# Unit 4's queries moved into unused columns of the MLP's hidden tile, and the hand-kept order of the first attention re-sorted

## The chip, the cores and the metric

The kernel runs on 1 core of one Trainium2 chip. The time is the device time of one execution in microseconds (us); a comparison takes the median of several runs. The engines are TensorE (PE; its weight loads, PEld, are listed apart), VectorE (DVE), ScalarE (ACT), GpSimd (POOL) and SyncE (SP), which here only issues DMA transfers. Each engine takes its instructions strictly in program order, and waits for other engines by semaphores.

## What is computed

Attention with normalized queries and keys for 8 batches of 12 heads (448 tokens, head size 64), then a layer norm and an MLP (multi-layer perceptron) with a residual, on 768 columns:

```python
def rmsnorm(x, g):
    return x / np.sqrt(np.mean(x * x, axis=-1, keepdims=True) + 1e-06) * g
q_n, k_n = rmsnorm(q, g_q), rmsnorm(k, g_k)
scores = q_n @ k_n.transpose(0, 1, 3, 2) / np.sqrt(64)
attn = softmax(scores)
x = (attn @ v)            # heads side by side: (8, 448, 768)
xn = (x - mean(x)) / np.sqrt(var(x) + 1e-06) * g_ln
out = x + np.maximum(xn @ w_ch1, 0.0) @ w_ch2     # 768 -> 3072 -> 768
```

## The kernel before

**Units, pairs, pieces.** Two heads make a pair, 48 pairs in all. Loads and preparation go by units of one or two pairs (`UNITS`): units 0 to 3 are batch 0 (pairs 0; 1; 2, 3; 4, 5), units 4, 5 and 6 are batch 1 (pairs 6, 7; 8, 9; 10, 11), unit 7 begins batch 2. The preparation of a unit is cut into pieces (`pieces`, from line 235), each one or a few instructions; their letters are

- `b`: takes the loaded tiles; `a`, `c`: squares of k and of q on ACT (L254); `d`, `e`: their sums by head on DVE (L257); `g`: the roots on ACT (L260, L261; `gq`, `gk` for unit 0)
- `i`: k times the gains (L271), on DVE for units 0 and 1 and on POOL after that; `j`: the high half of k in float16 (L277 on POOL for units 1 to 5, else L279 on ACT); `k`: the low half (L282, DVE)
- `l`: the scaled q (L79, DVE); `m`: its second copy (L318, POOL for units 1, 2 and 4, else DVE); `z`: the values in float16 (L324 and L330, POOL).

For a pair p, `Kp` and `Qp` transpose its keys and queries on PE into PSUM and copy them out (L360, L363, copy L365; L374, L377, copy L380 on ACT or L382 on DVE). From pair 6 on both use the one PSUM tile `tr`. `Sp.i` is one of seven score tiles (L397; L407 and L408 for the rest rows) with its exp on ACT (L413); the scores have two PSUM banks in turn. `Vp.i` multiplies such a tile with the values (L450, L452); `Vp.6` ends the pair, and DVE writes the pair's results (L465, L466, L467, L472). Pairs 1, 3 and 5 keep their sums in two of the three banks that the transposes of q, the first MLP products and psH use, too.

**The hand-kept list.** The first attention, batch 0 with the preparation of batch 1's first units and pair 6's scores, is written out by hand in `ORDER`, which `first_attention` goes through item by item. Since every engine runs in program order, this list is each engine's order. Besides the pieces it holds `Ln` (the loads of unit n, all on SP, keys first; `L8k` only the keys of unit 8), `Wn` (a third of the first weight matrix, w1, a DMA on POOL, L595), `G` and `G2` (the norm's gains), `Tp` (statistics, DVE, L625), `A`, `Nt`, `R` (aggregate, norm and root of the layer norm, L640 and L646), `Xt` (transposes of token tile t on PE, L682, copied by ACT, or by DVE for t = 2, L690), `Ut` (the first MLP products of token tile t, psU, L926; `U2` with the relu on ACT, L930) and `M` (seven small reductions on DVE).

**After the list** come the MLP of batch 0 (`first_mlp`: psH at L702, relu at L705, psC at L712) and, between its matmuls, the next batches' attention in steps that `attention` plans: the pieces of units 5 to 9 at the places in `EARLY`, less those that the list has already (`done`). `run_rest` spreads the steps evenly over the matmuls' cost. The step with unit 6's `b` also issues half of the second weight matrix.

**Buffers of the loads.** `load_unit` puts a unit's q, k and v either at a fixed place (`home`) or into one of three buffers of the pool `p_in` in turn. Fixed places lie in `hS`, the tile of the MLP's hidden layer, which nothing else uses before the MLP (4608 columns of float32; relu f writes columns 192 f to 192 f + 191), and in `free`, which is the tile `w2s` where the first batch's q and k were loaded. Before the change k4 and q4 take the first two buffers, k6 the third, and q6 the first one again, once `k4` has read it; `L8k` takes q4's. `RING` lists the tiles that go through the pool; the step that runs a unit's `k` or `l` loads the one three places on.

Of the kernel before, what the change touches and what calls it, by code (L numbers as in the profile page):

```python
# [22 lines left out]
UNITS = [(0, 0, 1), (0, 2, 1), (0, 4, 2), (0, 8, 2)]  # L23
# [10 lines left out]


ORDER = """
b0 a0 c0 L4 i0 j0 e0 k0 gq0 l0 b1 m0 a1 c1 K0 Q0 d0 G gk0 S0.0 S0.1 d1 e1 L5 i1 g1 j1 l1 k1 m1
z0 b2 a2 S0.2 d2 c2 S0.3 S0.4 K1 V0.0 e2 i2 S0.5 Q1 g2 l2 S0.6 S1.0 j2 V0.1 S1.1 S1.2 m2 b3
V0.2 a3 V0.3 k2 c3 S1.3 K2 V0.4 S1.4 z2 V0.5 Q2 S1.5 V0.6 V1.0 i3 W0 d3 e3 S1.6 V1.1 V1.2 S2.0
j3 T0 V1.3 S2.1 S2.2 Q3 V1.4 S2.3 K3 S2.4 V1.5 V1.6 S2.5 g3 z3 S2.6 V2.0 S3.0 S3.1 V2.1 k3  # L40
S3.2 b4 S3.3 V2.2 l3 a4 V2.3 m3 S3.4 V2.4 K4 S3.5 Q4 V2.5 V2.6 S3.6 Q5 S4.0 V3.0 S4.1 V3.1 i4
V3.2 d4 T1 K5 V3.3 W1 c4 V3.4 V3.5 S4.2 S4.3 V3.6 S4.4 S4.5 W2 e4 V4.0 V4.1 j4 S4.6 S5.0 k4
S5.1 g4 V4.2 l4 S5.2 V4.3 V4.4 V4.5 S5.3 K6 V4.6 z4 V5.0 S5.4 m4 b5 V5.1 G2 S5.5 L6 V5.2 S5.6
V5.3 V5.4 V5.5 Q6 a5 i5 V5.6 T3 T4 S6.0 S6.1 S6.2 S6.3 T5 S6.4 A V6.0 V6.1 N0 V6.2 N1 V6.3
S6.5 S6.6 d5 V6.4 X0 X1 U0 N2 R Q7 X2 c5 e5 j5 g5 k5 l5 z5 U1 U2 V6.5 M m5 V6.6 L7 L8k K7
""".split()
DMA_UNIT = 8
PE_SET = (DMA_UNIT + 1) % 2
# [15 lines left out]
TAIL = (11, 13, 17, 13, 17, 13, 19, 0)  # L64
FLAG_AT = (6, 30)
E_RING = 9
RING = [(u, n) for u in (4, 6, *range(DMA_UNIT, len(UNITS))) for n in "kq"]


def _rsqrt(nc, out, a, t, eps, mul=1.0):  # L70
# [17 lines left out]
class _Fast:  # L88
# [95 lines left out]
    def load_unit(self, u, which=(1, 0, 2)):  # L184
        nc = self.nc
        b, hs, m = UNITS[u]
        eng = nc.sync
        hS = self.hS.rearrange("p f n -> p (f n)").bitcast(FP32)
        home = {(4, 2): (hS, 0), (5, 0): (hS, 1920), (5, 1): (hS, 2816), (5, 2): (hS, 3712),
                (6, 2): (self.free, 3840), (7, 0): (self.free, 0), (7, 1): (self.free, 896),  # L190
                (7, 2): (self.free, 1792)}
        t = self.loads.setdefault(u, [None] * 3)
        for n in which:
            if (u, n) in home:
                x, c = home[u, n]
                t[n] = x[:, c:c + 896].rearrange("p (g d) -> p g d", d=D)
            else:
                t[n] = self.p_in.tile([128, 14, D], FP32, tag="kq", name="qk"[n])
            self.load_main(eng, n, t[n][:, 0:6 * m], b, hs, 2 * m)
            self.load_left(eng, n, t[n][:, 6 * m:7 * m], b, hs, 2 * m,  # L200
                           nc.gpsimd if (u, n) == (DMA_UNIT + 1, 1) else None)
# [327 lines left out]
    def attention(self):  # L529

        n, nu, nb0, done = B * NPAIR, len(UNITS), NPAIR, set(ORDER)
        todo = {}
        for u in range(4, nu):
            p, m = UNIT_PAIR[u], UNITS[u][2]
            if u == 4:
                continue
            plan = [(7 * (p - 4) + x, y) for x, y in PLAN]
            if u in EARLY:
                st, e = EARLY[u]
                names = ["bai", "d", "c", "e", "j", "gz", "k", "l", "m"]  # L540
                if u > DMA_UNIT:
                    names = ["bai", "d", "c", "j", "k", "e", "gz", "l", "m"]
                plan = [(st + (e - st) * x // 9, y) for x, y in enumerate(names)]
                if u >= DMA_UNIT:
                    plan += zip(TRANS_AT[u], "xyY")
            for at, names in plan:
                if self.late_v(u):
                    names = names.replace("z", "")
                todo.setdefault(at, []).extend(
                    self.prep_ops(u)[y] for y in names if y + str(u) not in done)  # L550
                for y in set(names) & set("kl"):
                    i = RING.index((u, "qk"[y == "k"])) + 3 if u != 5 and u != 7 else nu * 2
                    if i < len(RING):
                        todo.setdefault(at + (LOAD_AT[y == "l"] if u not in EARLY else 1), []).append(
                            lambda x=RING[i]: self.load_unit(x[0], ("qk".index(x[1]),)))
                if u in (6, 7) and "b" in names:
                    todo[at].append(lambda u=u: self.load_w2(u - 6))
        steps, mark = [], [0]

        for p in range(nb0, n + 1):  # L560
            for i in range(7):
                c = []
                if i == 0 and p < n and p % NPAIR == 0 and p > nb0:
                    c.append(lambda b=p // NPAIR: self.batch(b))
                c += todo.pop(7 * p + i, [])
                if p < n and f"S{p}.{i}" not in done and i < 6:
                    c.append(lambda p=p, i=i: self.scores(p, i))
                if p > nb0:
                    for x in {0: (), 1: (0, 1)}.get(i, (i,)):
                        if f"V{p - 1}.{x}" not in done:  # L570
                            c.append(lambda p=p, x=x: self.values(p - 1, x))
                if p < n and i == 6 and f"S{p}.6" not in done:
                    c.append(lambda p=p: self.scores(p, 6))
                if p > nb0 + 1 and i == 1 and (p - 1) % NPAIR:
                    c.append(lambda p=p: self.stats(p - 2))
                if p + 1 < UNIT_PAIR[DMA_UNIT]:
                    if i == 2 and f"K{p + 1}" not in done:
                        c.append(lambda p=p: self.trans_k(p + 1))
                    if i == 4 and f"Q{p + 1}" not in done:
                        c.append(lambda p=p: self.trans_q(p + 1))  # L580
                if p > nb0 and p % NPAIR == 0 and i == 6:
                    c.append(lambda p=p: self.stats(p - 1))
                if c:
                    steps.append(c)
            if p > nb0 and p % NPAIR == 0:
                mark.append(len(steps))
        return steps, mark
# [641 lines left out]
```

## Time and profile before

| | us |
|---|---|
| median of 3 runs (lowest, highest) | 590.16 (588.65, 591.14) |
| the profiled execution | 588.15 |
| its span from first to last instruction | 586.6 |
| PE busy in the span | 557.1 (95%) |
| DVE busy | 381.9 (65%) |
| ACT busy | 378.7 (65%) |
| POOL busy | 174.9 (30%) |

The profile is of one execution. Its own time is 1.55 us longer than the span, and 2.01 us shorter than the median of the runs. Busy time counts compute instructions only; the idle time before an instruction is shown in brackets with the engine that ended it. Rows in order of time give start, length, engine, line, operation and tiles; neighbouring instructions of a pipelined engine overlap by about 0.1 us in such rows. Lines are those of the kernel before; behind line 552 the changed kernel has one line more.

### The profile page before, as it was taken

How to read it: one execution, taken by the hardware profiler on the slowest of the kernel's cores; microseconds unless marked ns; L12 is line 12 of the kernel's file. 1: busy time of each engine (PE TensorE's matmuls, PEld its weight loads, DVE VectorE, ACT ScalarE, POOL GpSimd, SP SyncE). 2: the span in 40 equal slices, each digit the busy share in tenths (PEclk: the TensorE clock that was granted, in tenths of full speed). 3: DMA queues.
4: the chain of work that ended last, by engine and by line, in shares of the span. 5: the costliest groups of instructions: out<-in, count | busy, mean ns of one | idle time of the engine just before them, and what ended most of it. 6: DMA issues, size and time to landing. Idle time of an engine off the chain costs nothing.

```text
span 586.6 us, 13477 instructions
## 1 busy us (share of the span) xinstructions
PE 557.1 (95%) x5366; PEld 407.3 (69%) x5366; DVE 381.9 (65%) x832; ACT 378.7 (65%) x693; POOL 174.9 (30%) x196
## 2 busy tenths in 40 slices
PE   3777999999999999999999999999999999999995
PEld 1555566677677768777687768777787777777773
DVE  5898666699667586855757576854757744663434
ACT  5996887438786588647787489737787477323130
POOL 2854333303241520653141421643141400020000
PEclk9999999999999999999999999999999999999999
DMA  7999998948672796967753697958843480030201
GB/s 209 285 221 236 197 197 115 145 124 124 138 100 58 181 128 131 138 158 116 130 92 57 181 134 132 131 149 124 137 60 64 126 104 1 3 107 2 82 0 58
DMA packets 172664, 71.43 MB, mean 122 GB/s; under 512 B 132548, under 2 KB 167556, under 8 KB 172596
## 3 DMA queue, kind: packets, MB, share of 16 engines
q1 hardware_dynamic: 130100, 51.60, 41.8%
q0 software_dynamic: 41552, 18.29, 24.1%
q8 instruction: 43, 0.70, 0.5%
q10 hardware_dynamic: 944, 0.62, 0.4%
q14 instruction: 25, 0.20, 0.1%
HBM read 52.30 MB, written 11.01 MB: 108 GB/s over the span
## 4 chain that ended last, share of the span: by engine, by line
PE 78%; DVE 8%; ACT 3%; DMA 2%; issue 1%; SPq 0%; DVEq 0%; ACTq 0%
PE psH L779 30%; PE psP L802 28%; PE psS L397 7%; PE oA L450 4%; PE psH L702 3%; PE psC L712 2%; PE oB L452 2%; PE psS L403 1%; DVE w2s L745 1%; DMA q<-in_q_dram 1%; ACT E L413 1%; DVE stat L625 1%; DVE khl L282 1%; DVE ssq L257 1%; DVE x L467 1%
## 5 line engine op out<-in xcount | busy, mean ns | idle before, releaser
L413 ACT ACTIVATE E<-psS,rr_all 128x448 f16<-128x448 f32 x336 | 202.9, 634 | 41.3 <-PE psS L397 36.2
L779 PE MATMUL psH<-xnT,w 128*128 128x256 f16 (+1 forms) x2016 | 225.8, 261 | 0.0
L779 PEld LDWEIGHTS <-w 128*128 128x128 f16 x2016 | 172.7, 98 | 24.0 <-issue 4.8
L782 ACT ACTIVATE hS<-psH 128x512 f16<-128x512 f32 x150 | 90.0, 600 | 96.5 <-PE psH L779 92.1
L802 PEld LDWEIGHTS <-hS 128*128 128x128 f16 x1080 | 100.0, 98 | 57.5 <-issue 1.1
L802 PE MATMUL psP<-w,hS 128*128 128x384 f16 x672 | 126.8, 326 | 0.0
L397 PE MATMUL psS<-qU,kU 128*128 128x448 f16 x288 | 102.0, 356 | 9.4 <-ACT E L413 6.0
L450 PEld LDWEIGHTS <-E 128*128 128x128 f16 x1008 | 70.6, 98 | 37.2 <-issue 4.8
L271 POOL TENSOR_TENSOR k<-k,gprod 128x896 f32<-128x896 f32 x19 | 40.4, 2128 | 166.6 <-ACT khl L254 139.0
L785 DVE TENSOR_TENSOR hS<-hS 128x512 f16<-128x512 f16 (+1 forms) x119 | 56.8, 484 | 22.3 <-ACT hS L782 20.8
L802 PE MATMUL psP<-w2s,hS 128*128 128x384 f16 (+1 forms) x408 | 69.9, 321 | 0.0
L450 PE MATMUL oA<-v,E 128*128 128x65 f16 x864 | 66.7, 193 | 0.4 <-DVE x L467 0.4
L739 DVE SCALAR_TENSOR_TENSOR x<-psP,rs_all,x 128x384 f32<-128x384 f32 x60 | 36.4, 617 | 41.9 <-PE psP L802 41.2
L452 PE MATMUL oB<-v,E 128*128 128x65 f16 x288 | 51.8, 193 | 0.3
L813 POOL TENSOR_TENSOR x<-x,hS 128x384 f32<-128x384 f32 x21 | 23.4, 1127 | 84.4 <-ACT hS L881 83.8
L212 POOL DMA_DIRECT2D v<-in_v_dram x51 | 39.1, 781 | 8.9 <-PE oB L452 8.0
L397 PEld LDWEIGHTS <-kU 128*128 128x128 f16 x288 | 28.1, 98 | 16.8 <-issue 6.0
L465 DVE RECIPROCAL rec_all<-oA 128x6 f32<-128x6 f32 x48 | 9.2, 191 | 46.8 <-PE oA L450 46.7
L282 DVE TENSOR_TENSOR khl<-k,khl 128x896 f16<-128x896 f32 x19 | 20.7, 1091 | 25.9 <-ACT khl L279 25.9
L881 ACT ACTIVATE hS<-hS,rs_all 128x384 f32<-128x384 f32 x27 | 14.6, 604 | 33.1 <-DVE hS L785 33.1
L452 PEld LDWEIGHTS <-E 128*128 128x128 f16 x336 | 32.5, 97 | 0.4 <-DVE xl L472 0.4
L257 DVE TENSOR_REDUCE ssq<-khl 128x14 f32<-128x896 f32 (+1 forms) x24 | 25.5, 1062 | 6.0 <-ACT khl L254 5.0
(136 smaller groups left out, 601.0 us busy)
## 6 DMA issues: line engine op xcount, KB each, us to landing
k<-in_k_dram SPq DMA_DIRECT2D x19, 384.0 KB, 3.9
q<-in_q_dram SPq DMA_DIRECT2D x19, 384.0 KB, 4.2
out_dram<-x SPq DMA_DIRECT2D x14, 384.0 KB, 3.0
w<-in_moe_w_ch_dram POOLq DMA_DIRECT2D x3, 1536.0 KB, 15.0
w<-in_moe_w_ch_dram POOLq DMA_DIRECT2D x2, 2304.0 KB, 19.5
out_dram<-x POOLq DMA_DIRECT2D x9, 384.0 KB, 3.0
v<-in_v_dram POOLq DMA_DIRECT2D x51, 64.0 KB, 4.2
qU<-qn SPq DMA_TRANSPOSE x85, 2.5
```

What stands on the lines that cost most here:

```text
L212: nc.gpsimd.dma_start(out[:, :, j, 0:D], main[:, :, j])
L257: nc.vector.tensor_reduce(out=c["ssq"][:, n], in_=c["sq", n], axis=AX.X, op=ALU.add)
L271: (nc.vector if u in DVE_KG else nc.gpsimd).tensor_tensor(out=c["t"][1], in0=c["t"][1], in1=sh.gprod.unsqueeze(1).broadcast_to([128, g, D] ...
L397: nc.tensor.matmul(ps[0][:, 0:S], c["main"][:, ts(i, 128)], c["q"][:, ts(h, S)], start=True, stop=True)
L413: nc.scalar.activation(out=o, in_=x[:, 0:S], func=AFT.Exp, scale=self.units[u][3][:, g:g + 1], bias=EXP_BIAS)
L450: nc.tensor.matmul(oA[:, t, cs], E[:, ts(t, 128)], rhs, start=(i == 0 and t == 0), stop=(i == 6 and t == 2))
L452: nc.tensor.matmul(oB[:, cs], E[:, 320:448], rhs, start=(i == 0), stop=(i == 6))
L739: self.nc.vector.scalar_tensor_tensor(out=x, in0=ps, scalar=self.rs[:, b, t:t + 1], in1=x, op0=ALU.mult, op1=ALU.add)
L779: nc.tensor.matmul(ps[:, i], sh.w1[:, dc, ts(f + i, 128)], self.xnT[:, dc, 256 - N:256], start=(i == 0 and dc == 0), stop=(i == k - 1 and ...
L782: nc.scalar.activation(out=hT[:, f:f + k], in_=ps, func=AFT.Relu)
L785: nc.vector.tensor_tensor(out=out, in0=a, in1=c, op=op)
L802: nc.tensor.matmul(bank[x][:, c], a[:, f], w[:, f, c], start=(start and f == 0), stop=(stop and f == HALF - 1))
```

## The change

- The queries of unit 4 get a fixed place in `hS`, columns 896 to 1791, between v4 and q5. So only k4 of unit 4 goes through the pool, and k6 and q6 take the second and third buffer without a wait; `L8k` follows k4 in the first.
- `RING` loses its entry for q4, and the lookup in `attention` asks whether a tile is in `RING`.
- `ORDER` gets six more items, `b6 a6 c6 d6 e6 i6` near its end, and is re-sorted as a whole. Up to the first transposes little moves. Among other moves, `i1` stands ahead of `d0`; `a4` and `c4` come later; on POOL `z3` and `W0` come ahead of `i3`, and `z4` and `W2` ahead of `j4`; on DVE pair 3's results come after `k4`, `T3` and `T4` before pair 5's results, `e5` before `X2`; on PE `V5.0` comes right after `V3.6`, `U0` after `S6.6`, and `K7` right after `U2`.

The instructions are the same in number and kind; the steps after the list lack unit 6's six pieces, and one of them, left empty, is dropped.

```diff
 ORDER = """
-b0 a0 c0 L4 i0 j0 e0 k0 gq0 l0 b1 m0 a1 c1 K0 Q0 d0 G gk0 S0.0 S0.1 d1 e1 L5 i1 g1 j1 l1 k1 m1
-z0 b2 a2 S0.2 d2 c2 S0.3 S0.4 K1 V0.0 e2 i2 S0.5 Q1 g2 l2 S0.6 S1.0 j2 V0.1 S1.1 S1.2 m2 b3
-V0.2 a3 V0.3 k2 c3 S1.3 K2 V0.4 S1.4 z2 V0.5 Q2 S1.5 V0.6 V1.0 i3 W0 d3 e3 S1.6 V1.1 V1.2 S2.0
-j3 T0 V1.3 S2.1 S2.2 Q3 V1.4 S2.3 K3 S2.4 V1.5 V1.6 S2.5 g3 z3 S2.6 V2.0 S3.0 S3.1 V2.1 k3
-S3.2 b4 S3.3 V2.2 l3 a4 V2.3 m3 S3.4 V2.4 K4 S3.5 Q4 V2.5 V2.6 S3.6 Q5 S4.0 V3.0 S4.1 V3.1 i4
-V3.2 d4 T1 K5 V3.3 W1 c4 V3.4 V3.5 S4.2 S4.3 V3.6 S4.4 S4.5 W2 e4 V4.0 V4.1 j4 S4.6 S5.0 k4
-S5.1 g4 V4.2 l4 S5.2 V4.3 V4.4 V4.5 S5.3 K6 V4.6 z4 V5.0 S5.4 m4 b5 V5.1 G2 S5.5 L6 V5.2 S5.6
-V5.3 V5.4 V5.5 Q6 a5 i5 V5.6 T3 T4 S6.0 S6.1 S6.2 S6.3 T5 S6.4 A V6.0 V6.1 N0 V6.2 N1 V6.3
-S6.5 S6.6 d5 V6.4 X0 X1 U0 N2 R Q7 X2 c5 e5 j5 g5 k5 l5 z5 U1 U2 V6.5 M m5 V6.6 L7 L8k K7
+b0 a0 L4 i0 c0 j0 e0 gq0 b1 k0 l0 m0 a1 c1 K0 i1 G d0 Q0 gk0 S0.0 L5 d1 j1 z0 b2 S0.1 e1 S0.2 g1
+k1 a2 l1 d2 K1 S0.3 c2 e2 S0.4 S0.5 m1 i2 j2 Q1 V0.0 g2 S1.0 l2 m2 z2 S1.1 S0.6 b3 S1.2 V0.1 k2
+S1.3 V0.2 z3 V0.3 V0.4 K2 c3 V0.5 V1.0 S1.4 Q2 a3 S1.5 e3 V1.1 d3 V1.2 S1.6 V0.6 S2.0 W0 V1.3 i3
+S2.1 g3 V1.4 S2.2 Q3 K3 T0 S2.3 V2.0 j3 S2.4 V1.5 V1.6 V2.1 S2.5 V2.2 S2.6 b4 S3.0 l3 V2.3 S3.1
+k3 S3.2 m3 V2.4 S3.3 V3.0 c4 S3.4 V3.1 a4 i4 Q4 K4 V2.5 V2.6 S3.5 S3.6 Q5 S4.0 d4 K5 V3.2 S4.1
+S4.2 T1 W1 V3.3 S4.3 V4.0 V4.1 V4.2 S4.4 V3.4 V3.5 S4.5 z4 W2 S5.0 j4 e4 S4.6 S5.1 k4 g4 V3.6
+V4.3 V4.4 V5.0 S5.2 b5 S5.3 l4 V5.1 m4 V4.5 K6 G2 S5.4 V5.2 L6 a5 V5.3 V5.4 T3 S5.5 V4.6 V5.5
+S5.6 T4 Q6 V5.6 S6.0 S6.1 T5 A N0 N1 S6.2 V6.0 S6.3 i5 c5 V6.1 d5 S6.4 V6.2 X0 N2 V6.3 V6.4 X1
+Q7 S6.5 S6.6 U0 e5 X2 g5 M R j5 U1 V6.5 k5 U2 K7 l5 L7 L8k b6 m5 z5 a6 c6 d6 e6 V6.6 i6
 """.split()
-RING = [(u, n) for u in (4, 6, *range(DMA_UNIT, len(UNITS))) for n in "kq"]
+RING = [(4, "k")] + [(u, n) for u in (6, *range(DMA_UNIT, len(UNITS))) for n in "kq"]
...
-        home = {(4, 2): (hS, 0), (5, 0): (hS, 1920), (5, 1): (hS, 2816), (5, 2): (hS, 3712),
+        home = {(4, 0): (hS, 896), (4, 2): (hS, 0), (5, 0): (hS, 1920), (5, 1): (hS, 2816), (5, 2): (hS, 3712),
...
-                    i = RING.index((u, "qk"[y == "k"])) + 3 if u != 5 and u != 7 else nu * 2
+                    x = u, "qk"[y == "k"]
+                    i = RING.index(x) + 3 if x in RING else nu * 2
```

## The prediction

> **What bounds the kernel now.** I read the busy shares by stage first, then the chain of work that ended last, then TensorE's waits, and then, for the first 62 us, each engine's instructions in order of time. Columns by stage: length, then busy time of PE, PEld, DVE, ACT and POOL, the clock, the DMA share, GB/s; the third line is of PE alone.
>
> ```profile
> 23.00:55.34 32.34, 24.76 (x324) 16.81 (x322) 29.89 (x66) 27.56 (x52) 19.94 (x23) 1.00 1.11 231
> 12.00:32.40 20.40, 15.13 (x155) 9.21 (x154) 17.36 (x28) 19.87 (x38) 13.86 (x17) 1.00 1.09 273
> 57.30:580.00 522.70, 519.27 (x4926) 1.00 0.63 109
> ```
>
> From 57.3 to 580 us PE is busy 519.27 of 522.70: there the time is PE's work, which the change leaves alone, and at most 3.4 us of waits. Before that, in the first attention, PE is busy 24.76 of 32.34 and waits for others: ACT until about 32 us (19.87 of 20.40), DVE from 23 us on (29.89 of 32.34). The change re-sorts just this stage, so it can gain or lose only here and at the seam to the MLP (multi-layer perceptron). The chain shows the seam (start, length, engine, tile, line):
>
> ```profile
> 46.53 2.24 DVE stat L625 x9
> ...
> 49.17 1.96 DVE xn L646 x3
> ...
> 54.74 2.01 PE psU L926 x36
> ...
> 57.49 1.96 PE psH L702 x12
> ...
> 60.56 0.67 DVE kU L365
> ```
>
> After V5's results DVE does nine statistics, the norms, and the copies; PE does U1 and U2 (psU), and at 57.49 the MLP proper (psH) starts. Then it stops once more:
>
> ```profile
> 61.27 0.36 PE L397 MATMUL psS<-qU,kU 128*128 128x448 f16 x1 [1.35 <-DVE kU L365]
> ```
>
> S7.0 waited 1.35 us for the copy that belongs to K7, which came last in DVE's queue, behind M and V6's results.
>
> **The change part by part.**
>
> *The loads.* SyncE (SP) issues in order; q6 shared a buffer with k4:
>
> ```profile
> 29.28 1.75 SPq L150 DMA_DIRECT2D k<-in_k_dram  x2
> 41.48 0.37 SPq L142 DMA_DIRECT2D q<-in_q_dram  x1
> ```
>
> ```profile
> 58.89 0.94 ACT L254 ACTIVATE khl<-k 128x896 f32<-128x896 f32 x1
> ```
>
> From 31.03 (29.28 + 1.75) to 41.48 SP issued nothing. With unit 4's queries in hS, q6 goes out at about 31, v6 after k3 has read its place, and k7, q7, v7 behind them; k8 waits for k4's buffer in place of q4's. The number of DMAs is the same. Nothing on the path gains by it: unit 6's first square, at 58.89, stands directly behind the MLP's first relu and shows no wait for data. I cost the loads at 0: issued near 31 and used near 59, they have over 20 us in hand. What they could delay is a rival below.
>
> *Unit 6's first pieces in the list.* a6 and c6 move ahead of the MLP's first relu (two squares of 0.94), d6 and e6 ahead of V6's results (two reductions), i6 to the end of the list. ACT was not holding PE there, so the squares cost 0. The reductions delay V6's results and behind them K8's copy; Q8 needs K8's copy out of the same PSUM bank. Behind K7's copy stand l5, m5, d6, e6, V6's results and K8's copy: 1.1 + 0.4 + 2.0 + 1.33 + 0.57 = 5.4 us (prices below), while PE has 6 us of MLP and scores. The margin is about 0.4 us, so I take 0 and keep +0.5 as the upper end. One step without work falls out of the MLP's pacing, so S7.0 comes after 12 psH matmuls in place of 15.
>
> *K7 early.* K7 now follows U2, and its copy follows M and k5 on DVE. It is done about 2.3 us after X2's copy, S7.0 comes about 3.7 us after it. The wait goes: **-1.35**. S7.0's exps next wait for nothing but ACT, which is free.
>
> *The re-sorted list.* The prices, DVE first (start to next start is what one costs; the rows overlap a little):
>
> ```profile
> 32.33 0.66 DVE L365 COPY kU<-tr 128x960 f16<-128x960 f16 x1
> ...
> 36.49 1.07 DVE L625 BATCH_NORM_STATS2 stat<-x 128x6 f32<-128x256 f32 x3
> 37.48 0.64 DVE L365 COPY kU<-tr 128x960 f16<-128x960 f16 x1
> 38.04 0.18 DVE L465 RECIPROCAL rec_all<-oA 128x6 f32<-128x6 f32 x1
> ...
> 39.37 1.09 DVE L257 TENSOR_REDUCE ssq<-qn 128x14 f32<-128x896 f32 x1
> 40.37 1.08 DVE L282 TENSOR_TENSOR khl<-k,khl 128x896 f16<-128x896 f32 x1
> 41.37 1.09 DVE L79 SCALAR_TENSOR_TENSOR qn<-q,rr_all 128x896 f16<-128x896 f32 x1
> ...
> 53.57 0.62 DVE L382 COPY qU<-tr 128x896 f16<-128x896 f16 x1 [0.52 <-PE tr L377]
> 54.78 0.56 DVE L690 COPY w2s<-tr 128x768 f16<-128x768 f16 x1 [0.58 <-PE tr L682]
> ```
>
> A statistic like T1 costs 0.99 (36.49 to 37.48), a copy of K or Q 0.57, one pair's results 1.33 (38.04 to 39.37), e4 or k4 1.00. Now ACT and GpSimd (POOL):
>
> ```profile
> 28.76 2.76 ACT L413 ACTIVATE E<-psS,rr_all 128x448 f16<-128x448 f32 x5
> 31.42 0.94 ACT L254 ACTIVATE khl<-k 128x896 f32<-128x896 f32 x1
> ```
>
> ```profile
> 26.02 0.89 POOL L595 DMA_DIRECT2D w<-in_moe_w_ch_dram  x1
> ...
> 32.50 2.09 POOL L271 TENSOR_TENSOR k<-k,gprod 128x896 f32<-128x896 f32 x1 [3.30 <-issue]
> 34.53 1.72 POOL L595 DMA_DIRECT2D w<-in_moe_w_ch_dram  x2
> 36.73 0.93 POOL L277 CAST khl<-k 128x896 f16<-128x896 f32 x1 [0.48 <-DVE ssq L257]
> 37.60 0.83 POOL L324 CAST v<-hS 128x768 f16<-128x768 f32 x1
> 38.38 0.64 POOL L330 CAST vl<-hS 64x128 f16<-64x128 f32 x2
> ...
> 61.98 1.51 POOL L600 DMA_DIRECT2D w<-in_moe_w_ch_dram  x1
> ```
>
> Up to m3 both lists give DVE the same work, so it stands there at 32.3 (before, K4's copy starts at 32.33). In the new list Q4, K4, V2's results, Q5, d4, K5, T1, e4 follow: four copies, 1.33, 0.99 and two reductions, 6.6 us, and some 0.3 for Q4's transposes: 39.2. Next is k4, which needs j4 from GpSimd, and here the new list puts a **new wait**. The old queue on GpSimd is i4, W1, W2, j4, z4, the new one i4, W1, z4, W2, j4. i4 waits for a4 on ACT. a4 ended at 32.36 (31.42 + 0.94); the new list has one more exp (2.76 / 5 = 0.55) and c4 (0.84 to 0.94) ahead of it on a saturated ACT, and i1, now ahead of d0 on DVE at the very start, adds 0.1 to 0.6: about 34.0. Then 2.03 + 0.86 + 1.42 + 0.86 + 0.93: j4 ends at about 40.1, k4 starts at 40.3 in place of 39.2. Behind k4 on DVE stand V3's results, l4, K6's copy; PE's V5.0 waits for the PSUM bank of V3's results, and S5.2 behind it on PE, so ACT idles too, about 2 us, which it can afford.
>
> From k4's start to the end of X2's copy DVE took 14.97 us before (40.37 to 54.78 + 0.56). In the new list the same work stands there, plus V3's results (+1.33) and e5 (+1.00), while e5 and N2 fill the two idle gaps before Q7's and X2's copies (-0.52 - 0.58): 16.2. T3 and T4 move ahead of V5's results, but DVE has no hole to put them in, so this only exchanges places. X2's copy ends at 40.3 + 16.2 = 56.5, against 55.34. U1 covers the copy as before; U2 (half of 2.01), K7 and V6.6 (0.6) follow, and U0, now behind S6.6, adds up to 0.4: the MLP starts at about 58.5 in place of 57.49, **+1.0**. Bounds of this term: 0 if k4 isn't held (39.2), -1.3 if DVE's remaining idle time goes too (29.89 of 32.34 busy, less the 1.10 already taken), +2.9 if both weight issues on GpSimd take 1.51 as the one at 61.98 does (+1.3) and a4 is 0.6 later still.
>
> **Sum**: +1.0 - 1.35 + 0 = -0.35, with ends at -2.65 and +2.05. The profiled execution took 588.15 (span 586.6 and 1.55 around it), so 587.8; it ran 2.0 under the median of the runs, 590.16, so for the median **589.8**.
>
> **A rule against the change.** Weights and loads share the DMA engines:
>
> ```profile
> DMA to landing us min/median/max: 14.6/14.6/14.6
> ```
>
> This is W0, issued at 26.0 while SP's queue was idle from 31 to 41: it lands at 40.6. In the new list it is issued near 25.4, and U0, which needs it, runs some 2 us ahead of the end of X2's copy (X2's transposes and U0's own matmuls lie between), at about 54.5. The rule stands in the Trainium skill, DMA: Bandwidth & Descriptors, section Queues, rings and completion order: each engine takes turns between the queues that have work, a packet at a time. By that rule q6 to v7, now issued from 31 on, take up to half of every engine from W0. The trace agrees that the two queues ran side by side, but has no case of five loads against W0.
>
> **The rivals.**
>
> *A: k4 isn't held, and the list closes DVE's gaps.* For it: 2.45 us of DVE idle in the first row, and T4 before V5's results. Against it: z4 and W2 do stand ahead of j4. The MLP starts between -1.3 and 0, and the wait of 1.35 goes: -1.35 to -2.65, the median 587.5 to 588.8. Behind the seam PE's other waits (522.70 - 519.27 - 1.35 = 2.08) may shrink too, which would lead down to 586. Chance 0.24, of which 0.16 is faster by over 0.5%.
>
> *B (slower): GpSimd's queue holds k4 much longer.* Place: j4 behind z4 and both issues. From 40.3 on, each us that j4 is late is a us of the whole, since DVE, and by V5.0's bank PE and ACT, stand behind k4. For it: ACT is saturated ahead of a4, an issue has taken 1.51, and DVE's in-order queue has a new neighbour at every place. Against it: all other prices would have to hold too. At k4 = 42.2 the sum is +1.55, with K8's copy +2.05; from 43.1 on it is over +2.95 (593.1). Price +2 to +5, time 592 to 595. Chance 0.20, of which 0.17 is slower by over 0.5%.
>
> *C: the first weight piece lands late.* Place: U0 and, through it, X2 and the MLP's start. Doubling 14.6 gives 25.4 + 29.2 = 54.6, just when U0 wants it, and that is the point from which it costs anything; W1 and W2 follow in the same queue but are needed only five and thirteen chunks into the MLP. Price 0 to +4, time 590 to 594. Chance 0.06, of which 0.05 is slower by over 0.5%.
>
> *D: the move does nothing.* The buffer alone is without effect on the time (costed at 0), and if K7's wait is merely replaced by Q8 waiting for K8's copy (+0.5) and the DVE sum is as above, the result is 590.3. It is part of the forecast.
>
> **How the numbers follow.** Forecast, with D, 0.50, all of it within 0.5% (2.95 us, about what a measurement of this kernel can tell from no change); A 0.24; B 0.20; C 0.06. Faster by over 0.5%: 0.16, from A. Slower: 0.17 from B and 0.05 from C, 0.22. Within: 0.50 + 0.08 + 0.03 + 0.01 = 0.62. The range reaches from A's lower half, 587.0, to B's upper half, 594.5; about 0.1 lies below and 0.08 above. Between the ends of the forecast's own sum (-2.65 and +2.05) I take -0.35, since the wait at K7 and the order on GpSimd can be read off and the rest can't.
>
> **What would show it.** Right: S7.0 without the 1.35 wait; POOL's j4 (khl) ending near 40 and DVE idle about 1 us before k4; X2's copy ending near 56.5 and psH starting near 58.5; SP issuing q6 at about 31; PE from there on as before. Wrong: DVE never idle at k4 (A); psH after 60 (B); a PE wait on a DMA at U0 (C); a wait of Q8's transposes for DVE near 64.5. What would overturn the forecast is an engine that I held to be covered, above all ACT between S5.1 and X0.

## The result, and the profile after

| | median, us (lowest, highest) | runs |
|---|---|---|
| before | 589.32 (588.61, 591.37) | 22 |
| after | 590.70 (589.89, 591.93) | 22 |

The ratio after to before is 1.0021, 95% interval 1.0013 to 1.0030: a loss of 0.8 to 1.8 us, where a gain of 0.35 was forecast. The profiled execution of the changed kernel took 590.16 us, its span 588.6; that of before took 588.15 and 586.6.

The changed kernel's VectorE at the place of the new wait (start, length, engine, line, operation, tiles, and in brackets the idle time before and who ended it), then GpSimd's j4:

```profile
38.51 1.07 DVE L257 TENSOR_REDUCE ssq<-qn 128x14 f32<-128x896 f32 x1
40.54 1.09 DVE L282 TENSOR_TENSOR khl<-k,khl 128x896 f16<-128x896 f32 x1 [0.96 <-POOL khl L277]
...
44.75 0.66 DVE L365 COPY kU<-tr 128x960 f16<-128x960 f16 x1 [0.77 <-PE tr L363]
...
46.61 0.20 DVE L465 RECIPROCAL rec_all<-oA 128x6 f32<-128x6 f32 x1 [0.22 <-PE oA L450]
```

```profile
39.57 0.93 POOL L277 CAST khl<-k 128x896 f16<-128x896 f32 x1
```

j4 ends at 40.50 and k4 starts at 40.54 after 0.96 us of waiting, as forecast (40.1, 40.3, about 1). But two more idle times follow on VectorE, 0.77 and 0.22, and both wait for TensorE. TensorE's rows of the same stretch and of the seam:

```profile
42.59 0.20 PE L452 MATMUL oB<-v,E 128*128 128x65 f16 x1 [2.17 <-DVE x L467]
...
43.86 0.85 PE L363 MATMUL tr<-id,khl 128*128 128x128 f16 x6
...
59.27 2.11 PE L703 MATMUL psH<-w2s,w 128*128 128x384 f16 x12
...
65.76 0.35 PE L397 MATMUL psS<-qU,kU 128*128 128x448 f16 x1 [0.30 <-ACT E L413]
...
67.09 0.22 PE L374 MATMUL tr<-id,qn 128*128 128x128 f16 x1 [0.98 <-DVE kU L365]
```

V5.0 waited 2.17 us for the bank of V3's results. After that wait K6's six transposes took 0.85 us; in the profile of before they take 0.50:

```profile
41.58 0.50 PE L363 MATMUL tr<-id,khl 128*128 128x128 f16 x6
```

The clock tells why (the changed kernel's length, PE busy, clock, DMA share, GB/s):

```profile
39.20:42.60 3.40, 1.22 (x19) 1.00 1.14 239
42.60:46.00 3.40, 3.11 (x31) 0.51 1.13 215
```

After 3.40 us in which PE was busy 1.22, the granted clock was half for the next 3.40. The MLP starts at 59.27; the row of the same form stands at 57.33 in the profile of before (below). S7.0's wait of 1.35 us is gone, but Q8's first transpose now waits 0.98. The chain shows what stands before it (start, length, engine, tile, line), and GpSimd's row stands beside:

```profile
60.98 2.16 DVE qn L318
63.15 1.99 DVE ssq L257 x2
...
66.06 0.29 DVE xl L472
...
66.38 0.67 DVE kU L365
67.05 0.04 issue
67.09 0.22 PE tr L374
```

```profile
60.47 2.43 POOL L271 TENSOR_TENSOR k<-k,gprod 128x896 f32<-128x896 f32 x1 [2.84 <-issue]
```

m5 (L318) is a float16 copy that took 0.38 before; here it took 2.16. It lies beside i6 on GpSimd, which ends at 62.90; m5 ends 0.24 later. The two rows of before:

```profile
58.92 0.38 DVE L318 COPY qn<-qn 128x896 f16<-128x896 f16 x1
```

```profile
59.96 2.08 POOL L271 TENSOR_TENSOR k<-k,gprod 128x896 f32<-128x896 f32 x1 [4.77 <-issue]
```

Single profiles differ at their start. TensorE runs at half speed there, which the rows show (six transposes take 0.84 us) though the windows give a clock of 1.00, and this ends between 17 and 25 us, at another time in each execution. Here are before and then run e4 (below), whose lists agree up to this point:

```profile
22.71 0.50 PE L377 MATMUL psQ<-id,qn 128*128 128x128 f16 x6
```

```profile
23.75 0.83 PE L377 MATMUL psQ<-id,qn 128*128 128x128 f16 x6
```

So the clock time at which the MLP starts is no measure of a list. The expectations below count it from the first exp. ScalarE's and TensorE's rows of before, then ScalarE's of after:

```profile
12.05 1.16 ACT L413 ACTIVATE E<-psS,rr_all 128x448 f16<-128x448 f32 x2 [0.33 <-PE psS L397]
```

```profile
57.33 2.60 PE L702 MATMUL psH<-w2s,w 128*128 128x384 f16 x15
```

```profile
11.77 1.89 ACT L413 ACTIVATE E<-psS,rr_all 128x448 f16<-128x448 f32 x3 [0.24 <-PE psS L397]
```

That is 45.28 before and 47.50 after. But the slow stretch reaches past the first exp: the same count gives 46.26 for e4. A later mark is steadier: the sum of unit 4's q squares (piece e4), which is the last instruction of VectorE ahead of k4 (L257, `ssq<-qn`; 38.51 above, 39.37 before). From its start to the MLP's, before takes 17.96 us, e4 17.95, and the changed kernel 20.76. The two orders hold different work there (pair 3's results, 1.33, stand ahead of the mark before and behind it after), so this count compares only lists of the same order.

In these two profiles the MLP starts 1.94 us later (57.33 to 59.27), and from there to the end both take 529.3 us: the 1.35 gained at S7.0, and 0.64 at two later waits for exps, are used up by Q8 (0.98, and 0.30 for an exp ahead of it) and by waits further on, which differ between executions (TensorE's idle time from 50 us behind the MLP's start on is 1.2 us before, 1.6 here and 2.4 in e5, which has the list of before). The medians say 0.8 to 1.8, so these two single profiles overstate the difference.

### The profile page after: what moved, and what is told of

It reads as the page before. It is cut to its first block, busy times and chain, and to the rows that moved or that the text cites. A ratio compares the mean times of both kernels' runs of the same rounds, so it can differ in the third digit from the quotient of the medians.

```text
span 588.6 us, 13476 instructions
## 1 busy us (share of the span) xinstructions
PE 560.7 (95%) x5366; PEld 409.4 (70%) x5366; DVE 383.2 (65%) x832; ACT 378.5 (64%) x693; POOL 175.3 (30%) x196
## 4 chain that ended last, share of the span: by engine, by line
PE 76%; DMA 10%; DVE 7%; ACT 3%; SPq 2%; issue 1%; ACTq 0%; DVEq 0%
PE psH L780 30%; PE psP L803 27%; PE psS L397 6%; DMA w2s<-in_k_dram 4%; PE oA L450 4%; DMA k<-in_k_dram 4%; PE psH L703 2%; PE psC L713 2%; PE oB L452 1%; PE psS L403 1%; DVE w2s L746 1%; DMA q<-in_q_dram 1%; ACT E L413 1%; DMA hS<-in_k_dram 1%; SPq L150 1%
## 5 line engine op out<-in xcount | busy, mean ns | idle before, releaser
L397 PE MATMUL psS<-qU,kU 128*128 128x448 f16 x288 | 103.2, 362 | 7.4 <-ACT E L413 3.9
L450 PEld LDWEIGHTS <-E 128*128 128x128 f16 x1008 | 71.8, 99 | 40.0 <-issue 6.5
L450 PE MATMUL oA<-v,E 128*128 128x65 f16 x864 | 68.3, 196 | 1.5 <-ACT E L413 1.1
L882 ACT ACTIVATE hS<-hS,rs_all 128x384 f32<-128x384 f32 x27 | 14.6, 604 | 33.1 <-DVE hS L786 33.1
L452 PEld LDWEIGHTS <-E 128*128 128x128 f16 x336 | 32.8, 98 | 2.7 <-DVE x L467 2.3
L257 DVE TENSOR_REDUCE ssq<-khl 128x14 f32<-128x896 f32 (+1 forms) x24 | 25.5, 1062 | 5.0 <-ACT khl L254 4.5
## 6 DMA issues: line engine op xcount, KB each, us to landing
w<-in_moe_w_ch_dram POOLq DMA_DIRECT2D x3, 1536.0 KB, 14.9
```

What stands on the lines that cost most here:

```text
L257: nc.vector.tensor_reduce(out=c["ssq"][:, n], in_=c["sq", n], axis=AX.X, op=ALU.add)
L397: nc.tensor.matmul(ps[0][:, 0:S], c["main"][:, ts(i, 128)], c["q"][:, ts(h, S)], start=True, stop=True)
L450: nc.tensor.matmul(oA[:, t, cs], E[:, ts(t, 128)], rhs, start=(i == 0 and t == 0), stop=(i == 6 and t == 2))
L452: nc.tensor.matmul(oB[:, cs], E[:, 320:448], rhs, start=(i == 0), stop=(i == 6))
```

## The experiments

Runs are named e0 to e12. Pieces of the list have such names too; where one is meant, the text says piece. The diffs show only the part of a line that an edit touches; e5 has the change's edits to `RING` and the lookup too.

**Theory.** The loss has two places. First, k4 waits for j4; V3's results behind it hold TensorE for 2.2 us, the clock then falls to half, and VectorE waits for the slow transposes. Second, i6, which starts as soon as a6 is done, shuts m5 out, and K8's copy comes late for Q8. Against these stands the gain at K7. **Rivals:** the loads, issued 6 us earlier, compete for the DMA engines; or the re-sorted list costs by itself, wherever these two waits are.

Each ratio is to the kernel before, with its 95% interval. "First exp to MLP" and "mark to MLP" are the two counts above in that run's profile, "Q8" is the wait of Q8's first transpose there; where S7.0 still waits, the row says so.

| run | ratio | first exp to MLP, us | mark to MLP, us | Q8, us |
|---|---|---|---|---|
| before | 1 | 45.28 | 17.96 | none; S7.0 1.35 |
| after, and e0, the same again | 1.0021 [1.0013, 1.0030], 1.0021 [1.0010, 1.0033] | 47.50, 47.83 | 20.76, 20.70 | 0.98, 0.99 |
| e1, j4 first | 0.9982 [0.9971, 0.9993] | 45.56 | 18.65 | 0.99 |
| e2, c6 first | 0.9985 [0.9975, 0.9995] | 47.79 | 20.73 | none |
| e3, both | 0.9967 [0.9954, 0.9980] | 46.27 | 18.65 | none |
| e4, before with K7 early | 0.9970 [0.9959, 0.9982] | 46.26 | 17.95 | none |
| e5, before with the buffer | 1.0004 [0.9996, 1.0013] | 45.47 | 17.96 | none; S7.0 1.35 |
| e6, unit 6 not in the list | 1.0018 [1.0007, 1.0029] | 46.63 | 19.41 | none |
| e8, V3.6 ahead of k4 | 1.0009 [0.9998, 1.0019] | 46.25 | 19.44 | 0.98 |
| e9, e1 with V6's results beside i6 | 0.9972 [0.9957, 0.9987] | 46.48 | 18.65 | none |
| e10, S5.2 ahead of V5.0 | 1.0015 [1.0002, 1.0028] | 48.22 | 20.70 | 0.99 |
| e11, e3 with S5.2 ahead of V5.0 | 0.9956 [0.9939, 0.9974] | 45.54 | 18.66 | none |
| e12, e4 with unit 6's pieces | 0.9970 [0.9953, 0.9988] | 45.27 | 17.95 | none |

Profiles of one order spread by up to 1 us in the first count (45.27 to 46.26, 45.56 to 46.48) and by under 0.1 in the second.

**e1: j4 ahead of z4 and W2** in the changed kernel.

```diff
-S4.5 z4 W2 S5.0 j4 e4 S4.6
+S4.5 j4 z4 W2 S5.0 e4 S4.6
```

> The changed kernel with j4 ahead of z4 and W2 in the list, nothing else. Theory (the neighbours in the queues): the changed kernel's DVE stood idle 0.96 us for j4, PE 2.17 us for the bank of V3's results, and K6's transposes then ran at about half speed (0.85 in place of 0.50 us), which cost DVE another 0.77. With j4 early, k4 starts at about 39.5 in place of 40.54, PE's wait is about 1.1 us, and psH starts 1.0 to 1.9 us sooner than 59.27. Q8's wait of 0.98 us stays. Ratio to the kernel before 0.999 to 1.0005, from 1.0021. Rival (DVE is full anyway; the new order, with V3's results behind k4 and e5 ahead of X2, is what costs): the gap turns up again elsewhere, psH starts within 0.3 us of 59.27, ratio 1.0015 to 1.0025.

VectorE, then TensorE, of this run:

```profile
39.03 1.07 DVE L257 TENSOR_REDUCE ssq<-qn 128x14 f32<-128x896 f32 x1
40.01 1.08 DVE L282 TENSOR_TENSOR khl<-k,khl 128x896 f16<-128x896 f32 x1
```

```profile
42.05 0.20 PE L452 MATMUL oB<-v,E 128*128 128x65 f16 x1 [1.13 <-DVE x L467]
42.77 0.50 PE L363 MATMUL tr<-id,khl 128*128 128x128 f16 x6
```

k4 follows piece e4 without a bracket, TensorE's wait is half as long, the transposes take 0.50, and VectorE has no bracket from 38 to 56 us. From the mark to the MLP it is 2.1 us less, and the ratio falls by 0.0039, 2.3 us, more than expected. m5 still takes 2.16 and Q8 still waits. The first place is shown.

**e2: c6 ahead of a6**, so that i6 starts later. **e3: e1 and e2 together.**

```diff
-b6 m5 z5 a6 c6 d6 e6 V6.6 i6
+b6 m5 z5 c6 a6 e6 d6 V6.6 i6
```

> The changed kernel with c6 ahead of a6 and e6 ahead of d6, so that GpSimd's i6, which needs a6, starts about 0.85 us later, behind the start of m5 on DVE. Theory (m5 and i6 get in each other's way): in the changed kernel m5 took 2.16 us beside i6, before it took 0.38 with GpSimd idle; here m5 is back at 0.4 us or at most 0.9, K8's copy comes about 1.5 us sooner, and Q8's wait of 0.98 us goes. psH still starts at about 59.3. Ratio 1.0000 to 1.0010, from 1.0021. Rival (what delays K8's copy is d6 and e6 ahead of it, 2.0 us, whatever m5 takes): Q8's wait stays at 0.5 us or more, ratio 1.0015 to 1.0025.

> Both edits: j4 ahead of z4 and W2, and c6, e6 ahead of a6, d6. Theory: the two gains add, psH at 57.4 to 58.3, no wait of Q8, no wait of S7.0: ratio 0.9970 to 0.9990. Rival (the two waits share one slack, or the order itself costs): ratio 0.9995 to 1.0015.

VectorE, then GpSimd, of e2:

```profile
62.19 0.39 DVE L318 COPY qn<-qn 128x896 f16<-128x896 f16 x1
62.49 1.08 DVE L257 TENSOR_REDUCE ssq<-qn 128x14 f32<-128x896 f32 x1
```

```profile
62.51 2.08 POOL L271 TENSOR_TENSOR k<-k,gprod 128x896 f32<-128x896 f32 x1 [3.68 <-issue]
```

i6 lies beside a float32 sum now; both keep their normal length, m5 has its 0.39 again, and Q8's wait is gone. The second place is shown. The ratio falls by 0.0036, 2.1 us, more than expected and more than the 1.28 us of waits that went (0.98 and 0.30); with about 0.001 on either side of each ratio the rest can hardly be told from nothing. In e2 K6's transposes still took 0.85 us. Both repairs together gain 0.0054, less than the sum of the two points, 0.0075, but by the traces just what they should: 2.1 + 1.28 = 3.4 us, where 0.0054 is 3.2.

**e4: the kernel before with K7 ahead of V6.5**, nothing else.

```diff
-U1 U2 V6.5 M m5 V6.6 L7 L8k K7
+U1 U2 K7 V6.5 M m5 V6.6 L7 L8k
```

> The kernel before with K7 moved from the end of the list to right behind U2, nothing else. Theory (the wait at K7 is a term of its own): S7.0's wait of 1.35 us goes and psH starts as before, at about 57.4: 1.2 to 1.4 us faster, ratio 0.9976 to 0.9980. Rival (the wait moves on, to Q8's transposes or to an exp, as it did in the changed kernel): 0.4 us or less, ratio 0.9993 to 1.0000.

S7.0's wait goes, a wait of 0.26 for an exp appears at 65.55, and 0.0030 is 1.8 us, a little more than the 1.35; the interval holds both. One item moved gives as much as the whole change with both repairs (e3). So the rest of the re-sorting earns nothing that these runs can tell, and, since e3 is no slower than e4, it costs nothing that they can tell either once the two places are mended. That takes out the second rival.

**e0: the changed kernel again. e5: the buffer alone**, with the list of before.

```diff
-home = {(4, 2): (hS, 0),
+home = {(4, 0): (hS, 896), (4, 2): (hS, 0),
```

> The changed kernel once more, beside the next ones. Both theories: ratio 1.0005 to 1.0035 to the kernel before; TensorE's wait of about 2.2 us for V3's results and K6's transposes of 0.85 us again, if the cause lies in the order and not in one execution. If the 0.85 was an accident of the one profile, the transposes take 0.50 here and the MLP starts about 1 us earlier after the first exp (46.5 instead of 47.5 us).

> The list of before, with unit 4's queries in hS and the loads that follow from it. Theory (the loads are hidden by some 20 us of slack and take nothing from the weights' pieces): ratio 0.999 to 1.001, the wait of 1.35 us before S7.0 still there, W0 landing in about 15 us. Rival (five loads issued from 31 to 35 us on share the DMA engines with the weight pieces or with the loads just needed, and this is part of the loss of the change): ratio 1.001 to 1.003 and a wait of TensorE or VectorE for a DMA. Other side (the loads were late before): under 0.999.

e0 repeats the ratio, the 2.17 us and the 0.85 us. e5 is 1.0004, and its interval holds 1 and reaches 1.0013, 0.8 us; the time from the mark to the MLP is that of before. That takes out the first rival, the loads, as far as this interval goes.

**e6: unit 6's pieces out of the list.**

```diff
-L7 L8k b6 m5 z5 a6 c6 d6 e6 V6.6 i6
+L7 L8k m5 z5 V6.6
```

> The changed kernel without unit 6's pieces in the list (b6, a6, c6, d6, e6, i6 go back to the pacing of the MLP). Theory (the loss at Q8 comes from m5 sharing its time with i6, which starts as soon as a6 has ended): m5 0.39 us, no wait of Q8's first transpose for VectorE, while the wait for V3's results and the late MLP stay: ratio 0.9980 to 0.9995 to the kernel before, like the run with c6 first. Rival (d6 and e6 ahead of V6's results make the wait, whatever m5 takes): the wait goes here too, but then m5 needs not be short. Other rival (unit 6's pieces in the list were worth something later in the MLP): ratio 1.001 or more.

The mechanism came as expected (m5 0.39, no wait of Q8), the time did not: 1.0018. TensorE's rows of this run from 60 to 110 us that show a wait:

```profile
65.73 0.35 PE L397 MATMUL psS<-qU,kU 128*128 128x448 f16 x1 [0.25 <-ACT E L413]
77.66 0.38 PE L403 MATMUL psS<-qU,kU 128*64 128x448 f16 x2 [0.61 <-ACT E L413]
96.08 0.35 PE L397 MATMUL psS<-qU,kU 128*128 128x448 f16 x1 [0.31 <-ACT E L413]
```

The two later waits are those of the kernel before; the changed list had put one of 0.28 in their place. In sum 1.17 here stand against 0.98 + 0.30 + 0.28 = 1.56, so this edit is worth only 0.4 us (0.0007), which these intervals can't tell from nothing. The theory had left out what comes back; the other rival of the expectation had named it.

The same profile shows what the half clock costs. The wait at V5.0 was again 2.17, but here the clock stayed at 1.00 and VectorE waited only for j4. This run's windows, then its only bracket on VectorE from 38 to 56 us:

```profile
39.80:43.20 3.40, 1.22 (x19) 1.00 1.14 230
43.20:46.60 3.40, 2.56 (x36) 1.00 1.12 219
```

```profile
41.11 1.09 DVE L282 TENSOR_TENSOR khl<-k,khl 128x896 f16<-128x896 f32 x1 [0.66 <-POOL khl L277]
```

In the executions with half clock, VectorE's two later waits are 0.77 + 0.22 (after), 0.35 + 0.55 (e0) and 0.41 + 0.56 (e2), 0.9 to 1.0 us each time; in e6 none. From the mark to the MLP e6 takes 19.41 us against 20.70 to 20.76, 1.3 less. Of this, 0.3 is the shorter wait for j4 (0.66 against 0.96), so the half clock costs 1.0. The count from the first exp says less, since it takes in what the executions differ by ahead of the mark (in e6 and e3, for one, 3.4 us at half clock from near 21 us on). Why the clock did not fall at V5.0 in e6 is not shown. X2's copy, which ends VectorE's work for the MLP's start, in the changed kernel and then in e6:

```profile
57.05 0.55 DVE L691 COPY w2s<-tr 128x768 f16<-128x768 f16 x1
```

```profile
56.56 0.55 DVE L691 COPY w2s<-tr 128x768 f16<-128x768 f16 x1
```

**e8: V3.6 ahead of k4** in the changed kernel; GpSimd's queue stays.

```diff
-S5.1 k4 g4 V3.6
+S5.1 V3.6 k4 g4
```

> The changed kernel with V3.6 moved ahead of k4, so that V3's results (1.33 us of VectorE) fill the time in which k4 waits for j4; GpSimd's queue stays i4, W1, z4, W2, j4. Theory (k4's wait, and TensorE blocked behind k4 by the bank of V3's results, with the half clock that follows, make the late MLP): k4 waits 0 to 0.2 us, TensorE's wait at V5.0 falls from 2.2 to under 1.2 us, K6's transposes take 0.50 us, the MLP starts 1 to 2 us earlier after the first exp; ratio 0.9970 to 0.9995 to the kernel before (m5's wait at Q8 is still in it). Rival (GpSimd's order itself costs, since j4 and what follows it on VectorE come later whatever is done ahead of them): the MLP starts as late as in the changed kernel and the ratio stays at 1.0015 to 1.003.

VectorE of this run, then TensorE:

```profile
40.70 0.20 DVE L465 RECIPROCAL rec_all<-oA 128x6 f32<-128x6 f32 x1 [0.49 <-PE oA L450]
...
42.05 1.09 DVE L282 TENSOR_TENSOR khl<-k,khl 128x896 f16<-128x896 f32 x1
```

```profile
41.75 0.20 PE L452 MATMUL oB<-v,E 128*128 128x65 f16 x1 [0.69 <-DVE x L467]
43.20 0.23 PE L360 MATMUL tr<-id,khl 128*128 128x128 f16 x1 [0.62 <-DVE khl L282]
43.26 0.50 PE L363 MATMUL tr<-id,khl 128*128 128x128 f16 x6
```

The wait is split in two, the transposes run at full clock, and the MLP starts 1.3 us earlier after the mark than in e0, as the theory has it. The time gained only 0.0012, less than expected: VectorE still idles 0.49, and in this execution the clock fell later, after a stretch with many short waits (PE busy 1.82 of 3.40 us up to 50.4, with half clock from 50.2 to 53.6). Theory and rival are told apart by the MLP's start, hardly by the time.

**e9: e1, with V6.6's results ahead of m5, d6 and e6.**

```diff
-b6 m5 z5 a6 c6 d6 e6 V6.6 i6
+b6 z5 a6 c6 V6.6 m5 d6 e6 i6
```

> The run with j4 first, and V6.6's results moved ahead of m5, d6 and e6, so that V6's float32 results and not m5's float16 copy lie beside i6 on GpSimd. Theory (GpSimd's float32 operation and a float16 copy on VectorE shut each other out, VectorE's float32 operations do not): the four instructions of V6's results keep their 0.18, 0.17, 0.56 and 0.29 us, m5 takes 0.4 us or what is left of i6 plus 0.4, i6 about 2.1 us in place of 2.42; no wait of Q8's first transpose; ratio 0.9950 to 0.9980 to the kernel before. Rival (whatever of VectorE lies beside i6 is slowed, by traffic in the memory that both use): V6's results take 1 us or more longer in sum, Q8's wait stays, and the ratio stays at 0.9982 as with j4 first alone.

```profile
59.11 1.08 DVE L79 SCALAR_TENSOR_TENSOR qn<-hS,rr_all 128x896 f16<-128x896 f32 x1
60.11 0.19 DVE L465 RECIPROCAL rec_all<-oA 128x6 f32<-128x6 f32 x1
60.33 0.17 DVE L466 RECIPROCAL rec_all<-oB 64x2 f32<-64x2 f32 x1
60.53 0.56 DVE L467 TENSOR_TENSOR x<-oA,rec_all 128x384 f32<-128x384 f32 x1
61.11 0.29 DVE L472 TENSOR_TENSOR xl<-oB,rec_all 64x128 f32<-64x128 f32 x1
61.41 0.97 DVE L318 COPY qn<-qn 128x896 f16<-128x896 f16 x1
```

```profile
59.71 2.42 POOL L271 TENSOR_TENSOR k<-k,gprod 128x896 f32<-128x896 f32 x1 [2.84 <-issue]
```

V6's four instructions lie wholly beside i6 and keep their lengths. m5 starts 0.72 us before i6's end (59.71 + 2.42 = 62.13) and ends 0.25 after it, so it waited out just that rest. Q8's wait is gone, and 0.9972 lies in the theory's bounds; against the rival speak the lengths more than the ratio, whose interval includes 0.9982. One number missed: i6 took 2.42 and not 2.1. It starts 0.40 us before the instruction behind l5 (L79) does, and is longer by 0.34. So l5 kept i6 out as well; the other way round no run shows.

The Trainium skill, SBUF — State Buffer, section SBUF: two separate sides, has this rule: VectorE and GpSimd share one pair of ports, which is an exclusive lock for the length of an instruction; on VectorE's side it is taken by an operation in a two-port mode or, against a GpSimd operation that reads SBUF, as i6 does, by one with two SBUF inputs, and whichever engine starts first blocks the other fully. The traces agree as far as they go: the float16 copy waited for i6 and i6 for l5 (two tiles of SBUF), while the sums with one input (e2) and V6's results, which read a PSUM bank, kept their lengths.

**e10: S5.2 ahead of V5.0** in the changed kernel. **e11: the same in e3.**

```diff
-V4.3 V4.4 V5.0 S5.2 b5
+V4.3 V4.4 S5.2 V5.0 b5
```

> The changed kernel with S5.2 ahead of V5.0 on TensorE. VectorE, GpSimd and k4's wait of about 0.96 us stay as they are; TensorE has one score matmul pair inside its wait and ScalarE gets an exp in its idle 2.07 us. Theory (part of the late MLP is the half clock after a wait of 2.2 us, and not VectorE's wait): the clock stays at 1.00 from 40 to 50 us, K6's transposes take 0.50 us, the MLP starts 0.8 to 1.2 us earlier after the first exp than the 47.5 to 47.8 us of the changed kernel; ratio 1.0000 to 1.0015. Rival (VectorE's wait for j4 alone makes the late MLP, the half clock lies beside it): start at 47.5 to 47.8 us and ratio 1.0015 to 1.003. If the clock falls in spite of the matmuls, the run says nothing of its price.

> Both repairs (j4 ahead of z4 and W2; c6 ahead of a6) and S5.2 ahead of V5.0. Theory (TensorE's wait of 1.4 us at V5.0 is mostly beside VectorE's own work, which stays the same): 0.9955 to 0.9970 to the kernel before, at most 0.3 us better than both repairs alone (0.9967). Rival (ScalarE's idle time at this place was on the path): 0.5 to 1 us better, ratio 0.9945 to 0.9960.

e10's windows:

```profile
40.20:43.60 3.40, 1.53 (x20) 1.00 1.14 231
43.60:47.00 3.40, 3.09 (x35) 0.61 1.12 218
...
44.00:54.80 10.80, 9.34 (x84) 0.53 1.12 219
```

The clock fell in spite of the matmuls, and stayed at half from 44.4 to 54.6, 10.2 us. By its own condition the run says nothing of the price of half clock; it shows only that one score pair more ahead of the wait (1.86 us still) does not keep the clock up. e11's wait at V5.0 is 0.82 us, and its clock stays at 1.00. 0.9956 is the best of all versions by its point, but its interval covers both theory and rival, and e3's too. The traces speak for the theory: from the mark to the MLP e11 takes 18.66 us and e3 18.65, so the exp that ScalarE gets earlier brings nothing up to the MLP. That e11's MLP starts 0.7 earlier after the first exp lies ahead of the mark.

**e12: e4 with unit 6's pieces at the list's end**, c6 first.

```diff
-U1 U2 K7 V6.5 M m5 V6.6 L7 L8k
+U1 U2 K7 V6.5 M L7 L8k b6 m5 c6 a6 e6 d6 V6.6 i6
```

> The list of before with K7 ahead of V6.5 and with unit 6's first pieces (c6 ahead of a6) at its end; no new place for unit 4's queries, no re-sorting before U2. Theory (the re-sorted first attention brings nothing, and the first pieces save TensorE's waits for exps of 0.61 and 0.31 us near 77 and 96 us): K7's 1.35 us and up to 0.6 us more, ratio 0.9955 to 0.9970. Rival (the pieces cost as much on VectorE as they save, as where K8's copy has to wait behind them): 0.9970 to 0.9985, with a wait of Q8's transposes.

The waits near 77 and 96 us shrink from 0.61 and 0.31 to 0.28 and none, and Q8 has none. The span, 585.9, is the shortest of all, but the ratio is that of e4: 0.6 us is less than these intervals tell.

## Why the prediction was wrong

The measured 590.70 lies 0.9 above the forecast and inside its range; the direction is what was wrong. Two terms were too small, by 1.0 and by 1.28, with 0.64 coming back later: -0.35 + 1.0 + 1.28 - 0.64 = +1.3, which is within the measured 0.8 to 1.8.

- **Loads, 0:** right. q6 went out at 35.03 and not at 31, because one issue on SP took 5.47 us; nothing waited for it, and e5 is 1.0004. Rival C is out with that, and D's buffer is settled: no wait of TensorE for a DMA appears at U0, and W0 landed in 14.9 us (14.6 before), so nothing is seen of the halving that the rule against the change allowed.
- **K7 early, -1.35:** right. S7.0 waits no more, and e4 by itself gains 1.8 us.
- **k4 held by j4:** right, a wait of 0.96 against 1.1 (0.97 and 0.96 in e0 and e2, 0.66 in e6). That it started at 40.54 against 40.3 is partly luck: in e0 and e2 it was 41.55 and 41.77, as all of the stage lay later there. Rival A is out by the wait, and rival B too: it needed k4 at 42.2 or later, and a longer wait.
- **The MLP's start, +1.0: the step that failed first, by its size.** It measured +1.94 (57.33 to 59.27). The term in it that was too small is VectorE's time from k4's start to the end of X2's copy: 17.06 us (40.54 to 57.05 + 0.55), and 16.99 and 17.03 in e0 and e2, in place of 16.2. In e6, with the same list up to there and the clock at 1.00, it is 16.00 (41.11 to 56.56 + 0.55). So the list of the work was right, and the 1.0 on top are the two waits for TensorE at half clock. The prediction saw V5.0 blocked behind k4 and priced the stall as time that ScalarE can afford. It forgot that the blocked engine's own clock may fall: a wait of 2.17 us made the next 3.4 us of TensorE slow, and these held VectorE, which was the bound.
- **Unit 6's first pieces, 0 with +0.5 as the upper end: the step that failed second.** The list of what stands behind K7's copy was complete, 5.4 us against 6, with m5 at 0.4. m5 took 2.16, since i6, which the change moved into the list, runs beside it. That used the margin and cost 0.98 + 0.30; the later waits shrink by 0.6 for it. The prediction named GpSimd's queue for k4, and no rival for the place where GpSimd's work lies beside VectorE's. Rival D did name the place, Q8's wait instead of K7's, at +0.5, but put it down to the amount of work ahead of K8's copy and not to m5.
- **Rival B's sign** came true by other means than its own (j4 late, and DVE's queue behind it).

The Trainium skill, TensorE: Matmul & The Clock Gate, section What's actually happening, says that the clock falls after one idle window of some 3.4 us, and that the windows run freely, so the point varies with the phase. The traces fit the second half: of four executions with the same wait of 2.17 us three fell (after, e0, e2) and one did not (e6), and each low stretch lasted 3.4 us, or in e10 three times that. That the phase made the difference is not shown. The first half is too mild for this case: the clock fell after 3.40 us with PE busy 1.22 in the changed kernel and 1.82 in e8.

## What to carry to other kernels

Price a wait twice: by who waits behind it, and by what it does to the clock of a matmul engine that has little else to do just then. When a piece moves on GpSimd, look at what it will lie beside on VectorE, by kind of operation: here a float16 copy waited out the rest of it and an operation with two SBUF tiles held it up, while sums and PSUM reads did neither. And undo a re-sorted list in parts: here one moved item gave as much as the whole list with both repairs. To compare single profiles, count from a late mark that all of them share.

## What the runs showed of the hardware

A GpSimd multiply of 128x896 float32 (2.08 us) made a float16 copy on VectorE take 2.16 us in place of 0.38, and was itself stretched to 2.38 to 2.43 when VectorE's l5 was under way as it began. Half clock on TensorE lasted 3.4 us after one wait of 2.17 and 10.2 us in e10, whose wait was shorter (1.86); the 3.4 us cost 1.0. And the time from the program's start until TensorE runs at full speed for good differs by some us between executions with the same list up to there (0.50 for six transposes at 22.71 before, 0.83 at 23.75 in e4), so that two single profiles, counted from their starts, can't settle a difference of 1 us.
